# Window attention and softplus FFN: where the first block keeps its scores, and which engine forms the weights' lower parts

## The chip, the cores and the metric

The kernel runs on one core of one Trainium2 chip. The metric is device microseconds of one execution. Three runs of the kernel before gave a median of 1030.87 us (1030.74 to 1031.98).

## What is computed

Two stages follow each other. The first is attention over a window of 64 positions, for 8 batches, 8 heads, 576 positions and a head dimension of 64. The second is a feed-forward net (FFN) over the 4608 tokens, with 512 features and 2048 hidden units.

```python
scores = q @ k.transpose / sqrt(64)
scores = where((0 <= row - col) & (row - col < 64), scores, -1e9)
attn = softmax(scores)
x = (attn @ v) as [4608, 512]
h = x @ w_in
g = maximum(h, 0.0) + log1p(exp(-abs(h)))
out = (g @ w_out) as float32
```

The weights come as 64-bit floats, in 64-bit words.

## The kernel before, in words

**Blocks and pairs.** The 4608 tokens are worked on in 12 blocks of 384. In each block the attention is done for 4 head pairs (two heads of 64 make 128 features). The function `attention(g, hp)` is a generator: each `yield` ends a stage, and a list of events says at which point of the program the next stage is emitted. For the first two blocks (`by_pe`, L187) a stage list is: load q and k (L204, L206); load v (L226, L229); three score tiles, each a matmul (L254) and two masked copies with a row minimum on VectorE (L265); then, in one stage, the minimum over the two window ends (L271), six exponentials on ScalarE (L275), the sums' reciprocals (L280, L281), the scaling (L283), six transposes on TensorE (L290) and two copies out of PSUM (L291); then the product with v (L347), whose result is split into an upper part by ScalarE (L352) and a lower part by VectorE (L353). These two parts are `x`, what the FFN multiplies.

**Buffers of the first blocks.** The scores of a pair lie in the tile `st`, of which there are two (L246), so the third pair of a block can write its scores only when the first pair's transposes have read theirs. The k tiles (`kbd_s`), the v tiles (`v_ts`) and the two q tiles are also two each, taken in turn by `hp % 2`.

**Weights.** The 16 weight blocks (f = 0 to 15) are turned from 64-bit floats into a 32-bit value and then into an upper part `hi` and a lower part `lo` by `load_w(f)`: one DMA into `raws` (L166), ScalarE's |high word| scaled (L170), three bit operations on VectorE (L171, L172, L173), then for each of the two matrices ScalarE's rounded copy `hi` (L176) and GpSimd's difference `lo = w - hi` (L177). Blocks 0 to 11 take both matrices in one tile of 1024 elements per partition; blocks 12 to 15 take them one at a time, in tiles of 512. The tiles `raws` and `ws` of blocks 0 to 7 take turns in four pairs of spare buffers, `spare0` and `spare1`, `spare4` and `spare5`, `spare2` and `spare3`, `spare6` and `spare7`; blocks 8 to 11 use two of the pairs. Later the same spare buffers hold the finished parts of blocks 8 to 15.

**FFN.** A step (g, f) is `ffn_up` (12 matmuls L401, ScalarE L405 to L407, VectorE L409, L411, L412) and `ffn_down` (9 matmuls L422). The order of the passes is block 0 with f = 0 to 7, block 1 with all f, block 0 with f = 8 to 15, then blocks 2 to 11 with all f. After the first pass block 0's sum is put away in DRAM (`part`) through the tiles that also bring the last weight blocks in.

**Order of the work.** Each event has a number, and the events are emitted in the order of these numbers: the step n stands at 2n + 0.5 and 2n + 5.5, `load_w(f)` at `CONVERT[f]`, and a pair's stages at `BASE[g] + PACE[g] * hp` plus the offsets of `STG0` (blocks 0 and 1) or `STG` (the others). Up to event 100 the order on each engine's queue is not that of emission: a planner plays the program through with its own costs and takes, on each engine and on SP's DMA queue, the earliest emitted instruction that is ready in its simulated time. From event 100 on TensorE's order is that of emission. Whatever the plan, each queue then runs in its order on the chip.

```python
CONVERT = (-104, -98, -93, -88, -6, -3, 0, 3, 6, 8, 11, 13, 16, 18, 21, 24)
BASE = (-100, -10, 24)
PACE = (5, 4, 7)
STG0 = (-4.5, 0.5, 1, 2, 3, 4, 7, 8)
...
            if f == loaded:
...
    events.sort(key=lambda e: e[0])
```

**Start.** GpSimd zeroes parts of the k and v tiles (L115 to L118, L123: ten memsets), then builds the masks and the identity matrix (L127 to L146).

Of the kernel before, what the change touches and what calls it, by code (L numbers as in the profile page):

```python
# [8 lines left out]
F32 = mybir.dt.float32  # L9
# [4 lines left out]
ALU = mybir.AluOpType  # L14

P = 128
TB = 384
NJ = TB // P
WIN = 64
BIG = 1.0e9  # L20
CH = 64
# [1 line left out]

SPLIT = 8
DOWN = 5.5
CONVERT = (-104, -98, -93, -88, -6, -3, 0, 3, 6, 8, 11, 13, 16, 18, 21, 24)
BASE = (-100, -10, 24)
PACE = (5, 4, 7)
STG0 = (-4.5, 0.5, 1, 2, 3, 4, 7, 8)
# [10 lines left out]
def window_attention_softplus_ffn(  # L40
# [24 lines left out]
    nc = tc.nc  # L65
# [13 lines left out]
    att = ctx.enter_context(tc.tile_pool(name="att", bufs=1))  # L79
# [12 lines left out]
    NE = NF // 2  # L92
    w_first = [[cpool.tile([P, NE, DM], F32R, name=f"w{m}{i}") for i in range(2)] for m in range(2)]
    w_last = {}

    def spare(k, shape, dtype, name):
        return late.tile(shape, dtype, name=name, tag=f"spare{k}")

    def weight(m, i, f):

        if f < NE:
            return w_first[m][i][:, f, :]
        k = (f - NE) // 4
        if (m, i, k) not in w_last:
            w_last[m, i, k] = spare(4 * k + 2 * m + i, [P, 4, DM], F32R, f"w{m}{i}{k}")
        return w_last[m, i, k][:, f % 4, :]


    W = CH + P
# [2 lines left out]

    kbd_s = [att.tile([P, 2, CH + TB], F32, name="kbd", tag=f"k{i}") for i in range(2)]
    for t in kbd_s:
        nc.gpsimd.memset(t[D:P, 0, :], 0.0)  # L115
        nc.gpsimd.memset(t[0:D, 1, :], 0.0)
        nc.gpsimd.memset(t[0:D, 0, 0:CH], 0.0)
        nc.gpsimd.memset(t[D:P, 1, 0:CH], 0.0)  # L118

    v13 = cpool.tile([P, NCH, 2, 2, D], BF16, name="v13")  # L120
    v_ts = [att.tile([P, 2, NJ, P], F32, name="v_t", tag=n) for n in ("nat", "tr")]
    for t in v_ts:
        nc.gpsimd.memset(t[0:CH, 0, 0, :], 0.0)  # L123

# [23 lines left out]
    def load_w(f):  # L150


        if f < NE + 4:
            k = (0, 4, 2, 6)[f % 4] if f < NE else (4, 6)[f % 2]
            parts = [(spare(k, [P, 2, DM], w_words.dtype, "raws"), spare(k + 1, [P, 2, DM], F32, "ws"), 0, 2)]
        else:
            parts = [
                (
                    ff.tile([P, 1, DM], w_words.dtype, name="raw"),
                    att.tile([P, 1, DM], F32, name="wh", tag=("v_in", "v12")[m]),  # L160
                    m, m + 1,
                )
                for m in range(2)
            ]
        for raw, w, m0, m1 in parts:
            nc.sync.dma_start(raw, w_words[f][:, m0:m1, :])  # L166
            words = raw.bitcast(U32).rearrange("p m (n two) -> p two m n", two=2)
            low, high = words[:, 0, :, :], words[:, 1, :, :]
            wb = w.bitcast(U32)
            nc.scalar.activation(w, high.bitcast(F32), AF.Abs, scale=REBIAS)  # L170
            nc.vector.tensor_scalar(wb, wb, 3, None, ALU.logical_shift_left)  # L171
            nc.vector.scalar_tensor_tensor(wb, high, 0x80000000, wb, ALU.bitwise_and, ALU.bitwise_or)  # L172
            nc.vector.scalar_tensor_tensor(wb, low, 29, wb, ALU.logical_shift_right, ALU.bitwise_or)  # L173
            for m in range(m0, m1):
                hi, lo = [weight(m, i, f) for i in range(2)]
                nc.scalar.copy(hi, w[:, m - m0, :])  # L176
                nc.gpsimd.tensor_tensor(lo, w[:, m - m0, :], hi.bitcast(F32), ALU.subtract)  # L177


    xs = {}  # L180
# [2 lines left out]
    def attention(g, hp):  # L183
# [59 lines left out]
            nc.vector.tensor_tensor(k_lo, k_in, k_hi.bitcast(F32), ALU.subtract)  # L243
        yield

        st = att.tile([P, 2, NJ, W], F32, name="st", bufs=2)  # L246
        mn = att.tile([P, 2, NJ], F32, name="mn", bufs=2)
        sm = att.tile([P, 2 * NJ], F32, name="sm", bufs=2)
        for j in range(NJ):
# [12 lines left out]
            t = ORDER[g] * NJ + j  # L262
            m = mask_c if (t * P) % S == 0 else mask_b if (t * P) % S + P > S else mask
# [191 lines left out]
    for g in range(NB):  # L455
        for hp in range(NP):
            if g < 3:
                base = BASE[g] + PACE[g] * hp
            else:
                base = 2 * NF * (g - 1) + SHP * hp + SH  # L460
            stages = attention(g, hp)
            for at in STG if g >= 2 else STG0:
                events.append((base + at, lambda stages=stages: next(stages, None)))
    loaded = 0
    for n, (g, f, first, last) in enumerate(steps):
        if f == loaded:
            events.append((CONVERT[f], lambda f=f: load_w(f)))
            loaded += 1
        events.append((2 * n + 0.5, lambda g=g, f=f: ffn_up(g, f)))
        events.append((2 * n + DOWN, lambda step=steps[n]: ffn_down(*step)))  # L470
# [52 lines left out]
```

## Time and profile before

| | |
|---|---|
| median of 3 runs | 1030.87 us |
| the profiled execution, its own time | 1030.02 us |
| its span in the profile | 1028.2 us |
| TensorE (PE) busy | 974.8 us, 95% of the span |
| VectorE (DVE) busy | 802.6 us, 78% |
| ScalarE (ACT) busy | 742.0 us, 72% |
| GpSimd (POOL) busy | 61.8 us, 6% |
| granted TensorE clock, mean over the span | 0.976 of full |

The profile is of one execution. A row of a group view names the line, the engine, the operation and the tiles, then the busy time, the mean duration, and the idle time just ahead on that engine with what ended it. A row of a timeline gives start and duration, both in us. A row of windows gives, for one stretch of time, the busy time of each engine with its number of instructions, then the granted TensorE clock as a share of full speed and the DMA's share and rate.

### The profile page before, as it was taken

How to read it: one execution, taken by the hardware profiler on the slowest of the kernel's cores; microseconds unless marked ns; L12 is line 12 of the kernel's file. 1: busy time of each engine (PE TensorE's matmuls, PEld its weight loads, DVE VectorE, ACT ScalarE, POOL GpSimd, SP SyncE). 2: the span in 40 equal slices, each digit the busy share in tenths (PEclk: the TensorE clock that was granted, in tenths of full speed). 3: DMA queues.
4: the chain of work that ended last, by engine and by line, in shares of the span. 5: the costliest groups of instructions: out<-in, count | busy, mean ns of one | idle time of the engine just before them, and what ended most of it. 6: DMA issues, size and time to landing. Idle time of an engine off the chain costs nothing.

```text
span 1028.2 us, 16614 instructions
## 1 busy us (share of the span) xinstructions
PE 974.8 (95%) x5888; PEld 859.1 (84%) x5888; DVE 802.6 (78%) x1775; ACT 742.0 (72%) x1705; POOL 61.8 (6%) x56
## 2 busy tenths in 40 slices
PE   4559889999999999999999999999999999999998
PEld 2337778988888998998899899899989899889997
DVE  6998587797987888878878878878878887874332
ACT  5467477787877788778778778778878877865443
POOL 5365020000000000000000000000000000000000
PEclk8679989999999999999999999999999999999999
DMA  8662253375554456444444534534634635521000
GB/s 295 229 219 71 88 149 83 83 186 123 126 121 114 113 114 130 117 113 116 131 103 117 140 91 118 151 83 113 164 83 113 161 86 104 141 49 32 31 1 31
DMA packets 203155, 119.05 MB, mean 116 GB/s; under 512 B 130880, under 2 KB 195136, under 8 KB 201536
## 3 DMA queue, kind: packets, MB, share of 16 engines
q1 hardware_dynamic: 203072, 118.00, 45.4%
q8 instruction: 46, 0.75, 0.3%
q14 instruction: 37, 0.30, 0.1%
HBM read 76.28 MB, written 10.22 MB: 84 GB/s over the span
## 4 chain that ended last, share of the span: by engine, by line
PE 85%; DVE 9%; DMA 2%; ACT 1%; issue 1%; SPq 1%; DVEq 0%; ACTq 0%
PE ps_o L422 37%; PE ps_h L401 37%; PE ps_a L376 5%; PE ps_a L258 5%; DVE ws L172 2%; DVE ws L173 1%; DVE st L265 1%; DVE st L283 1%; DMA raws<-in_w_words_dram 1%; DVE ws L171 1%; DVE st L271 0%; DMA tr<-nat 0%; ACT st L275 0%; PE ps_a L254 0%; DVE sm L280 0%
## 5 line engine op out<-in xcount | busy, mean ns | idle before, releaser
L401 PE MATMUL ps_h<-x,w 128*128 128x384 f32 x2304 | 445.3, 340 | 7.6 <-ACT x L352 3.9
L422 PE MATMUL ps_o<-w,g 128*128 128x512 f32 x1728 | 435.5, 395 | 0.0
L401 PEld LDWEIGHTS ps_h<-x,w 128*128 128x128 f32 x2304 | 402.6, 189 | 22.5 <-ACT x L352 5.2
L422 PEld LDWEIGHTS ps_o<-w,g 128*128 128x128 f32 x1728 | 318.0, 188 | 57.7 <-ACT g L411 0.3
L405 ACT ACTIVATE u<-ps_h 128x384 f32<-128x384 f32 x192 | 93.9, 490 | 121.8 <-PE ps_h L401 118.8
L409 DVE SCALAR_TENSOR_TENSOR u<-ps_h,u 128x384 f32<-128x384 f32 x192 | 106.4, 554 | 70.5 <-ACT u L407 69.2
L275 ACT ACTIVATE st<-st,mn 128x128 f32<-128x128 f32 x288 | 111.9, 390 | 19.3 <-DVE st L271 19.3
L412 DVE TENSOR_TENSOR g<-u,g 128x384 fp32r<-128x384 f32 x192 | 106.6, 555 | 10.5 <-ACT g L411 8.6
L265 DVE CUSTOM_DVE_ANT_0 st<-ps_a,mask 128x192 f32<-128x192 f32 x216 | 69.4, 351 | 57.9 <-PE ps_a L258 45.4
L407 ACT ACTIVATE u<-u 128x384 f32<-128x384 f32 x192 | 100.3, 523 | 4.2
L406 ACT ACTIVATE u<-u 128x384 f32<-128x384 f32 x192 | 100.7, 526 | 3.2
L258 PE MATMUL ps_a<-k,q_hl 128*128 128x192 f32 x480 | 76.5, 283 | 0.0
L376 PEld LDWEIGHTS <-v 128*128 128x128 bf16 x1088 | 56.1, 98 | 22.9 <-issue 21.8
L376 PE MATMUL ps_a<-tr,v 128*128 128x128 bf16 (+1 forms) x1088 | 72.0, 213 | 0.2
L258 PEld LDWEIGHTS ps_a<-k,q_hl 128*128 128x128 f32 x480 | 66.6, 192 | 4.1 <-issue 0.5
L411 ACT CAST g<-u 128x384 fp32r<-128x384 f32 x112 | 57.0, 509 | 14.2 <-DVE u L409 13.5
L306 ACT CAST nat<-st 128x768 bf16<-128x768 f32 x40 | 33.2, 831 | 40.0 <-DVE st L304 40.0
L275 ACT ACTIVATION_READ_ACCUMULATOR st<-st,mn 128x1 f32 x288 | 53.9, 187 | 0.0
L381 ACT COPY xf<-ps_a 64x384 f32<-64x384 f32 x80 | 38.1, 477 | 20.3 <-PE ps_a L376 19.2
L283 DVE TENSOR_TENSOR st<-st,sm 128x768 f32<-128x768 f32 x48 | 47.6, 991 | 1.5
L382 DVE TENSOR_TENSOR xf<-ps_a,xf 64x384 f32<-64x384 f32 x80 | 43.9, 548 | 5.2 <-ACT xf L381 4.0
L325 DVE TENSOR_TENSOR v_in<-v_in,v 128x896 f32<-128x896 f32 x40 | 43.5, 1086 | 4.7 <-ACT v L324 4.7
(80 smaller groups left out, 868.0 us busy)
## 6 DMA issues: line engine op xcount, KB each, us to landing
k_in<-in_kT_dram SPq DMA_DIRECT2D x80, 224.0 KB, 3.9
v_in<-in_v_dram SPq DMA_DIRECT2D x80, 224.0 KB, 3.6
q_in<-in_qT_dram SPq DMA_DIRECT2D x84, 192.0 KB, 4.1
raws<-in_w_words_dram SPq DMA_DIRECT2D x12, 1024.0 KB, 6.0
out_dram<-raw SPq DMA_DIRECT2D x12, 512.0 KB, 2.8
raw<-in_w_words_dram SPq DMA_DIRECT2D x8, 512.0 KB, 4.3
out_dram<-raw SPq DMA_DIRECT2D x12, 256.0 KB, 2.6
v_t<-in_v_dram SPq DMA_DIRECT2D x16, 96.0 KB, 3.8
```

What stands on the lines that cost most here:

```text
L258: mm(spv[:, hh, :], q_hl[:, hh, js], part[:, hh, kc], start=(hh == 0 and i == 0), stop=(hh == 1 and i == 1), skip_group_check=True,)
L265: nc.vector.tensor_tensor_reduce(st[:, hh, j, :], spv[:, hh, :], m, QSCALE, 3.0e38, ALU.add, ALU.min, mn[:, hh, j : j + 1])
L275: nc.scalar.activation(sv[:, i, 0:P], sv[:, i, 0:P], AF.Exp, bias=mn[:, hh, j : j + 1], scale=-1.0, accum_out=sm[:, i : i + 1])
L283: nc.vector.tensor_tensor(pn, pn, sm.unsqueeze(2).to_broadcast([P, 2 * NJ, P]), ALU.mult)
L376: mm(av[:, osl], (v13 if s else v12)[:, c, hh, :, :], src, start=(i == 0), stop=(i == len(passes) - 1), skip_group_check=True,)
L401: mm(hv, weight(0, a, f)[:, c * P : (c + 1) * P], x[b][c], start=(i_mm == 0), stop=(i_mm == 3 * NC - 1))
L405: nc.scalar.activation(u, hv, AF.Abs)
L406: nc.scalar.activation(u, u, AF.Exp, scale=-1.0)
L407: nc.scalar.activation(u, u, AF.Ln, bias=1.0)
L409: nc.vector.scalar_tensor_tensor(gf, hv, 0.0, u, ALU.max, ALU.add)
L412: nc.vector.tensor_tensor(gt[1], gf, gt[0].bitcast(F32), ALU.subtract)
L422: mm(ops[g][j], gt[a][:, js], weight(1, b, f), start=(first and i == 0), stop=(last and i == 2),)
```

## The change

Four things are done.

- In block 0 each head pair gets a score tile of its own. The tiles are the spare buffers 0, 4, 2 and 6, the ones into which the raw words of weight blocks 0 to 3 are then loaded.
- So `load_w(0)` to `load_w(3)` are emitted later, each just behind the stage that reads the last scores of the pair whose buffer it takes (pair 0's at -96, the load at -95.5, and so on).
- The lower parts of all 16 weight blocks are formed by VectorE instead of GpSimd: 32 subtractions of 128x512.
- The ten memsets of the k and v tiles are issued on VectorE instead of GpSimd.

```diff
-CONVERT = (-104, -98, -93, -88, -6, -3, 0, 3, 6, 8, 11, 13, 16, 18, 21, 24)
+CONVERT = (-95.5, -90.5, -85.5, -80.5, -6, -3, 0, 3, 6, 8, 11, 13, 16, 18, 21, 24)
...
+    FIRST = (0, 4, 2, 6)
+
...
     for t in kbd_s:
-        nc.gpsimd.memset(t[D:P, 0, :], 0.0)
-        nc.gpsimd.memset(t[0:D, 1, :], 0.0)
-        nc.gpsimd.memset(t[0:D, 0, 0:CH], 0.0)
-        nc.gpsimd.memset(t[D:P, 1, 0:CH], 0.0)
+        nc.vector.memset(t[D:P, 0, :], 0.0)
+        nc.vector.memset(t[0:D, 1, :], 0.0)
+        nc.vector.memset(t[0:D, 0, 0:CH], 0.0)
+        nc.vector.memset(t[D:P, 1, 0:CH], 0.0)
...
     for t in v_ts:
-        nc.gpsimd.memset(t[0:CH, 0, 0, :], 0.0)
+        nc.vector.memset(t[0:CH, 0, 0, :], 0.0)
...
-            k = (0, 4, 2, 6)[f % 4] if f < NE else (4, 6)[f % 2]
+            k = FIRST[f % 4] if f < NE else (4, 6)[f % 2]
...
-                nc.gpsimd.tensor_tensor(lo, w[:, m - m0, :], hi.bitcast(F32), ALU.subtract)
+                nc.vector.tensor_tensor(lo, w[:, m - m0, :], hi.bitcast(F32), ALU.subtract)
...
-        st = att.tile([P, 2, NJ, W], F32, name="st", bufs=2)
+        if g == 0:
+
+            st = spare(FIRST[hp], [P, 2, NJ, W], F32, "st0")
+        else:
+            st = att.tile([P, 2, NJ, W], F32, name="st", bufs=2)
```

## Rows read from the trace of the kernel before

**Rows 1.** Windows over the whole span: busy time of each engine, clock, DMA.
```profile
0.00:97.00 97.00, 56.01 (x276) 38.15 (x277) 83.87 (x156) 55.60 (x140) 51.77 (x50) 0.79 0.65 213
97.00:135.00 38.00, 32.38 (x201) 26.86 (x199) 22.76 (x60) 19.50 (x55) 3.16 (x2) 0.95 0.30 94
135.00:200.00 65.00, 62.88 (x346) 55.92 (x347) 50.65 (x115) 50.73 (x116) 6.84 (x4) 0.97 0.43 104
...
200.00:1028.00 828.00, 823.52 (x5072) 738.21 (x5069) 645.31 (x1448) 616.13 (x1396) 0.00 (x0) 1.00 0.45 106
```

**Rows 2.** The chain that ended last, cut to 0 to 130 us, by line.
```profile
by line: DVE ws L172 14.7%; DVE ws L173 11.8%; PE ps_o L422 8.0%; PE ps_h L401 6.7%; DVE st L265 6.5%; issue 6.1%; DVE st L283 5.5%; DMA raws<-in_w_words_dram 5.2%; DVE ws L171 4.4%; PE ps_a L254 3.1%; DVE sm L280 3.1%; DMA part<-raw 2.8%; 
```

**Rows 3.** Timeline: the ends of the two blocks' attention, and the third pair's scores.
```profile
25.74 1.65 PE L254 MATMUL ps_a<-kbd,k_in 128*128 128x384 f32 x2
...
69.56 0.54 DVE L353 TENSOR_TENSOR x<-ps_o,x 128x384 fp32r<-128x384 f32 x1
...
134.46 0.45 ACT L352 CAST x<-ps_a 128x384 fp32r<-128x384 f32 x1
```

**Rows 4.** Timeline of TensorE: the first pair's scores, transposes and product with v.
```profile
4.50 4.18 PE L254 MATMUL ps_a<-kbd,k_in 128*128 128x384 f32 x6 [4.50 <-DMA kbd<-in_kT_dram]
...
22.83 1.51 PE L290 MATMUL ps_a<-ident,st 128*128 128x128 f32 x6 [7.85 <-ACT w L176]
24.27 1.54 PE L347 MATMUL ps_a<-pt,v_t 128*64 128x64 f32 x12
```

**Rows 5.** VectorE's groups by shape, 0 to 100 us.
```profile
L172 DVE SCALAR_TENSOR_TENSOR ws<-raws,ws 128x1024 uint32<-128x1024 uint32 x12 | 20.0, 1666 | 0.0
L173 DVE SCALAR_TENSOR_TENSOR ws<-raws,ws 128x1024 uint32<-128x1024 uint32 x12 | 16.1, 1338 | 0.0
L171 DVE TENSOR_SCALAR ws<-ws 128x1024 uint32<-128x1024 uint32 x12 | 11.9, 995 | 1.6 <-ACT ws L170 1.6
L283 DVE TENSOR_TENSOR st<-st,sm 128x768 f32<-128x768 f32 x6 | 7.3, 1221 | 0.1
...
L280 DVE TENSOR_SCALAR sm<-sm 128x6 f32<-128x6 f32 x6 | 4.2, 708 | 2.0 <-ACT st L275 2.0
```

**Rows 6.** Timeline of VectorE: single instructions, all but the last with GpSimd idle.
```profile
10.37 0.69 DVE L171 TENSOR_SCALAR ws<-ws 128x1024 uint32<-128x1024 uint32 x1 [1.61 <-ACT ws L170]
...
11.53 1.22 DVE L172 SCALAR_TENSOR_TENSOR ws<-raws,ws 128x1024 uint32<-128x1024 uint32 x1
...
17.18 0.17 DVE L280 TENSOR_SCALAR sm<-sm 128x6 f32<-128x6 f32 x1
...
25.52 0.94 DVE L283 TENSOR_TENSOR st<-st,sm 128x768 f32<-128x768 f32 x1
...
48.77 0.68 DVE L173 SCALAR_TENSOR_TENSOR wh<-raw,wh 128x512 uint32<-128x512 uint32 x1
...
71.11 2.28 DVE L172 SCALAR_TENSOR_TENSOR ws<-raws,ws 128x1024 uint32<-128x1024 uint32 x1
```

**Rows 7.** GpSimd: the window of its subtractions alone (L177), and two single rows.
```profile
0.00:100.00 100.00, 45.27 (x26) 0.80 0.63 207
...
69.49 2.82 POOL L177 TENSOR_TENSOR w<-ws,w 128x512 fp32r<-128x512 f32 x2 [2.49 <-ACT w L176]
93.63 1.29 POOL L177 TENSOR_TENSOR w<-wh,w 128x512 fp32r<-128x512 f32 x1
```

**Rows 8.** Timeline: the last memsets of the tiles on GpSimd, and VectorE's first instruction.
```profile
3.24 0.34 POOL L123 MEMSET v_t<- 64x128 f32 x2
...
7.56 0.36 DVE L265 CUSTOM_DVE_ANT_0 st<-ps_a,mask 128x192 f32<-128x192 f32 x1 [7.56 <-POOL mask_b L145]
```

**Rows 9.** SP's queue: one stretch in which it waits with two weight loads.
```profile
20.79 8.79 SPq L166 DMA_DIRECT2D raws<-in_w_words_dram  x2
```

**Rows 10.** From VectorE's last bit operation to GpSimd's subtraction, and the page's exponentials.
```profile
73.43 1.22 DVE L173 SCALAR_TENSOR_TENSOR ws<-raws,ws 128x1024 uint32<-128x1024 uint32 x1
...
75.38 2.94 POOL L177 TENSOR_TENSOR w<-ws,w 128x512 fp32r<-128x512 f32 x2 [3.07 <-ACT w L176]
...
L275 ACT ACTIVATE st<-st,mn 128x128 f32<-128x128 f32 x288 | 111.9, 390 | 19.3 <-DVE st L271 19.3
```

## The prediction

> **What bounds the kernel now.** I read the windows first. From 200 us on TensorE is busy 823.5 of 828 us at full clock, so nothing the change touches there can matter: all of it works in the first 200 us. There TensorE is busy 56.0 of 97, 32.4 of 38 and 62.9 of 65 us, part of it at a clock of 0.79 [rows 1]. The reader is to see that in the first stretch VectorE carries 83.9 of 97 us and TensorE waits. The chain says the same: up to 130 us its largest shares are VectorE's three bit operations on the weights (L172, L173, L171: 30.9% together) and the masks and scaling of the scores [rows 2].
>
> The order is the second thing to see. Block 0's x is complete only at 69.56 + 0.54 = 70.1 us, block 1's at 134.46 + 0.45 = 134.9 (its last lower part a little later) [rows 3]. Block 0's third pair scores at 25.74 us, right behind pair 0's transposes and product with v (22.83 to 25.8) [rows 3, 4], as two score tiles demand. VectorE fills that time with weights: by 100 us it has done 12 blocks' bit operations and GpSimd 26 subtractions, that is blocks 0 to 12, while the first pass needs 0 to 7 [rows 5, 7].
>
> **The subtractions.** Nothing in the trace shows this subtraction on VectorE. The nearest row is a 128x512 operation with two SBUF inputs of 32 bits: 0.68 us [rows 6]; below lies 0.17, the fixed price of a tiny operation, above 0.94, a subtraction-like operation of 768 elements [rows 6]. I take 0.68, the same shape and number of inputs. By 100 us that is 26 x 0.68 = 17.7 us, by 135 us 28 of them, 19.0 us. (The bounds make 28 cost 5 to 26 us.)
>
> What it frees: beside GpSimd's subtractions VectorE's own instructions are longer. L172 takes 1.22 us with GpSimd idle, and 2.28 at 71.11, while GpSimd's pair of subtractions runs from 69.49 to 72.31 [rows 6, 7]. The excess of the group means over such single rows is 12 x (1.666 - 1.22) = 5.4 for L172, 12 x (1.338 - 1.22) = 1.4 for L173, 12 x (0.995 - 0.69) = 3.7 for L171, 6 x (1.221 - 0.94) = 1.7 for L283, 6 x (0.708 - 0.17) = 3.2 for L280 [rows 5, 6]: 15.4 us, and groups not shown can only add. So the trade is nearly even on VectorE, 3.6 us dearer by 135 us.
>
> The Trainium skill, page SBUF — State Buffer, section Who interferes with whom, says that VectorE and GpSimd share a pair of ports as an exclusive lock, and that the one that comes second blocks for the whole instruction. By that rule I estimate a gain of up to 26 x 1.29 = 33.5 us of VectorE time instead of 15.4, which would make the sum some 18 us better; the trace agrees on single instructions, which lose 1.06 us, and not on the sum.
>
> GpSimd loses too: its subtractions take 45.27 / 26 = 1.74 us each, against 1.29 for one late in the stretch [rows 7]. The waiting is split between the two, and I keep the measured 15.4.
>
> **The memsets.** Ten memsets leave GpSimd, where the last two end at 3.58 us; VectorE waits for GpSimd's masks until 7.56 [rows 8]. VectorE has nothing else to do then, so they cost nothing there as long as that cover lasts (if it is gone, at most the 3.58 us within which all ten ran on GpSimd). GpSimd's masks come earlier by up to as much; TensorE's first score tile is there from about 4.50 + 4.18 / 6 = 5.2 us [rows 4], so VectorE may start at 5.2 instead of 7.56: 2.4 us gained, bounds 0 and 2.4.
>
> **The score tiles and the later weight loads.** With four tiles the third and fourth pair no longer wait for the transposes of the first two. What they wait for next is TensorE: a pair takes 4.18 + 1.51 + 1.54 = 7.2 us in the early rows [rows 4], so four pairs take 29, and x of block 0 can't be complete before about 4.5 + 29 + 1 = 34 us. With a couple of weight blocks on VectorE in between (1.22 + 1.22 + 0.69 + 2 x 0.68 = 4.5 us each) I expect 40 to 45, against 70. The raw words of blocks 0 to 3 load only after the transposes of their pair, so conversion starts near 17 us instead of 9: harmless while VectorE has attention to do, and I put 4 us of new idle time on it. The loads stand in SP's queue, where v and k loads can be stuck behind them, as happened for 8.79 us before [rows 9]; this wait is now for transposes rather than for conversions, and I cost it at nothing beyond those 4 us.
>
> An earlier x does not by itself shorten the front, since VectorE must do its work first. So the sum runs over VectorE, to the state "block 1's x complete and the first pass done", 135 us now. Busy time up to there 83.87 + 22.76 = 106.6 [rows 1]; minus 15.4, plus 19.0: 110.2. Idle time up to there is 13.1 + 15.2 = 28.4. The 15.2 fall after 97 us, when TensorE runs the whole first pass as one lump and VectorE has nothing pressing; with x of block 0 some 28 us earlier the first pass spreads out beside the conversion, and I take 3 of them as left. The 13.1 become 13.1 - 2.4 + 4, and I add 3 for subtractions that wait for ScalarE's `hi` (below). That is 20.7 of idle time and a state at 130.9: 4 us gained.
>
> The rest comes from order. Weight blocks 8 to 13 were done before this state and are not needed for it; they crowded in because attention was blocked. Six blocks are 27 us of VectorE. I take half as postponed, 13.5 us, and they have a place: from 135 to 200 us VectorE is idle 14.3 of 65 us [rows 1]. The state then lies at 117.4, 17.6 us earlier, and from there on TensorE is the bound as now. The profiled execution took 1030.02 us, 0.85 below the median of the runs shown; 1030.0 - 17.6 = 1012.4, or 1013 against the median. With none postponed it is 1027, with all of them 1000.
>
> **The rivals.**
> - *More than that.* All six blocks are postponed and the conversion of later ones fits under the second pass: 31 us, 1000 (988 to 1003 with the clock's share, which stands at 0.79 in the first 97 us [rows 1]). Against it: 27 us don't fit in the 14.3 of idle time. Or half are postponed, as forecast, and each of GpSimd's subtractions had held VectorE up for its whole 1.29 us [rows 7]: 26 x 1.29 - 15.4 = 18.1 us more, 1013 - 18 = 995. For this speaks L172's 2.28, against it that the group means show an excess of 15.4 only. Chance 0.13 together, little of it the second. By the rule of the Trainium skill's page SBUF — State Buffer cited above it would be the second.
> - *It evens out.* The scores come early but the planner still lets the weights crowd in, or weight loads in SP's queue hold up the loads of pairs 2 and 3. VectorE is then only 3.6 us dearer and starts 2.4 earlier: 1026 to 1035, about 1031. For it: 8.79 us of such a stretch in the trace [rows 9]; against it: pair 2's matmuls waited with TensorE idle 7.85 us just ahead of the transposes [rows 4]. Chance 0.17.
> - *VectorE waits for ScalarE, slower.* GpSimd waited for `hi` at no cost; VectorE, with everything queued behind, does not. L173 ends at 74.65 and the subtraction could start at 75.38, 0.73 us later, with ScalarE free [rows 10]. Where `hi` stands behind a pair's six exponentials it is 6 x 0.39 = 2.3 us more [rows 10]. Over 14 blocks the mechanism decides from 17.6 / 14 = 1.3 us a block; at 2 us a block it costs 28 against 17.6, 1041, at 3 us 1055. Behind the waiting subtraction stand masks and scaling of the next pairs, for which TensorE waits. Against it: the planner knows this dependency and places other work between. Chance 0.18.
>
> **How the numbers follow.** The forecast has 0.52, with a range of its own from 1003 to 1026. About 0.2%, 2 us, is what a measurement of this kernel can tell from no change. Faster is the forecast, the larger gain and a part of the even case: 0.52 + 0.13 + 0.05 = 0.70. Same is 0.07 of the even case. Slower is 0.05 of it and the 0.18: 0.23. For 8 in 10 the range takes in the forecast, the better end to 998 (0.04), the even case, and the slower one up to 1036, a wait of about 1.6 us a block (0.07).
>
> **What would show it.** Right: no L177 on GpSimd; L172 close to 1.22 us in the mean and L280 near 0.17; 32 subtractions of about 0.68 us on VectorE; block 0's third pair scoring before pair 0's transposes, x of block 0 complete before 45 us; block 1's x near 117; blocks 8 to 13 partly converted after that. Wrong: x of block 1 still near 135, with VectorE as busy; VectorE idle ahead of the subtractions, ended by ScalarE's L176, beyond some 18 us in all; or ScalarE long idle ahead of L170 for raw words that come late.

## The result, and the profile after

The changed kernel takes 1034.1 us (median of 20 runs, 1028.98 to 1039.08), the kernel before 1031.26 (20 runs, 1029.9 to 1032.73): a ratio of 1.0027, 95% interval 1.0014 to 1.0039. It is slower by about 3 us where 1013 was forecast. Lines from `def spare` on stand 2 further down in the new file, those from `st` on 6.

The engines' busy time on the page of the changed kernel (1035.78 us, span 1034.0):

```profile
PE 982.4 (95%) x5888; PEld 867.2 (84%) x5888; DVE 802.4 (78%) x1817; ACT 741.9 (72%) x1705; POOL 3.9 (0%) x14
```

GpSimd's work is gone but for 3.9 us (61.8 before). TensorE runs the same 5888 matmuls but is busy 7.6 us longer, so it idles 51.6 us of its span against 53.4 before. What was lost is not idle time but clock (0.970 of full in the mean of the span, 0.976 before). The windows (columns as in [rows 1]) show where:

```profile
0.00:97.00 97.00, 70.94 (x354) 51.74 (x355) 81.14 (x199) 57.39 (x146) 3.94 (x14) 0.82 0.65 213
97.00:135.00 38.00, 24.01 (x127) 19.60 (x126) 29.01 (x59) 19.90 (x51) 0.00 (x0) 0.76 0.41 116
135.00:200.00 65.00, 59.83 (x319) 52.95 (x318) 44.71 (x105) 46.84 (x111) 0.00 (x0) 0.96 0.38 94
```

Up to 97 us TensorE does 354 matmuls instead of 276: the early score tiles work. From 97 to 135 it does 127 instead of 201, at a granted clock of 0.76 instead of 0.95. So by 135 us the two kernels stand even, with 481 matmuls and 477 before; it is from 135 to 200 us that the changed kernel falls behind, with 319 matmuls instead of 346. VectorE is busy 81.14 + 29.01 = 110.15 us by 135 us; the forecast's sum, before anything is postponed, said 110.2. The two blocks' last parts of x, on VectorE's timeline:

```profile
55.20 0.55 DVE L359 TENSOR_TENSOR x<-ps_o,x 128x384 fp32r<-128x384 f32 x1
...
133.40 0.56 DVE L359 TENSOR_TENSOR x<-ps_a,x 128x384 fp32r<-128x384 f32 x1 [0.69 <-ACT x L358]
```

Block 0's x is complete 14 us earlier than before (55.8 against 70.1), block 1's only 1.5 us (134.0 against 135.5). VectorE's groups, 0 to 135 us, answer to [rows 5]:

```profile
L179 DVE TENSOR_TENSOR w<-ws,w 128x512 fp32r<-128x512 f32 x24 | 15.6, 681 | 0.7 <-ACT w L178 0.7
L175 DVE SCALAR_TENSOR_TENSOR ws<-raws,ws 128x1024 uint32<-128x1024 uint32 x12 | 14.6, 1216 | 0.0
L174 DVE SCALAR_TENSOR_TENSOR ws<-raws,ws 128x1024 uint32<-128x1024 uint32 x12 | 14.5, 1215 | 0.0
L173 DVE TENSOR_SCALAR ws<-ws 128x1024 uint32<-128x1024 uint32 x12 | 8.2, 687 | 4.1 <-ACT ws L172 4.0
...
L173 DVE TENSOR_SCALAR wh<-wh 128x512 uint32<-128x512 uint32 x6 | 2.5, 424 | 4.7 <-ACT wh L172 4.7
L286 DVE TENSOR_SCALAR sm<-sm 128x6 f32<-128x6 f32 x8 | 1.3, 163 | 5.3 <-ACT st L281 5.3
```

The prices are the forecast ones: the subtraction 0.68 us, the bit operations 1.22 and 0.69, the tiny L286 0.16. The subtractions (L179) wait 0.7 us for ScalarE in all, so the slower rival's mechanism did not occur. Much of the idle time, 8.7 us, stands ahead of L173 instead, where VectorE waits for ScalarE's first step on the weights. ScalarE's waits up to 135 us (total, times, longest) say for what:

```profile
ACT ws L172 <- DMA raws<-in_w_words_dram: 10.6, 6, 4.6
...
ACT wh L172 <- DMA raw<-in_w_words_dram: 7.3, 4, 4.4
```

That is 17.9 us for raw words not yet there; before it was 8.5 + 3.2 = 11.7. What stands behind such a wait in ScalarE's queue waits too. Two places on ScalarE's timeline, at the third pair of block 0 and the fourth of block 1:

```profile
41.95 1.12 ACT L172 ACTIVATE ws<-raws 128x1024 f32<-128x1024 f32 x1 [4.62 <-DMA raws<-in_w_words_dram]
42.97 0.47 ACT L297 COPY pt<-ps_a 128x384 f32<-128x384 f32 x1
...
129.31 0.66 ACT L172 ACTIVATE wh<-raw 128x512 f32<-128x512 f32 x1 [4.44 <-DMA raw<-in_w_words_dram]
129.88 0.46 ACT L297 COPY pt<-ps_a 128x384 f32<-128x384 f32 x1
```

And TensorE's timeline at the same two places, the transposes (L296) and the product with v (L353) that needs their copy:

```profile
37.67 1.49 PE L296 MATMUL ps_a<-ident,st 128*128 128x128 f32 x6
...
43.49 1.54 PE L353 MATMUL ps_a<-pt,v_t 128*64 128x64 f32 x12 [3.06 <-ACT pt L297]
...
125.06 1.51 PE L296 MATMUL ps_a<-ident,st 128*128 128x128 f32 x6 [6.22 <-DVE st L289]
130.39 2.46 PE L353 MATMUL ps_a<-pt,v_t 128*64 128x64 f32 x24 [3.82 <-ACT pt L297]
```

The copy of the transposed scores could have run at about 39 and 126.5 us, where the transposes end. It stood behind a weight block that was still loading, and TensorE idled 3.06 and 3.82 us for it. The Trainium skill, page Perfetto Trace Analysis, section Tensor Engine Instruction (MATMUL, LD_WEIGHTS), says that ScalarE and VectorE execute strictly first in, first out; these rows agree.

### The profile page after: what moved, and what is told of

Same layout as the page of the kernel before. It is cut to its first block, busy times and chain, and to the rows that moved or that the text cites. A ratio compares the mean times of both kernels' runs of the same rounds, so it can differ in the third digit from the quotient of the medians.

```text
span 1034.0 us, 16622 instructions
## 1 busy us (share of the span) xinstructions
PE 982.4 (95%) x5888; PEld 867.2 (84%) x5888; DVE 802.4 (78%) x1817; ACT 741.9 (72%) x1705; POOL 3.9 (0%) x14
## 4 chain that ended last, share of the span: by engine, by line
PE 88%; DMA 4%; DVE 4%; ACT 2%; issue 1%; SPq 0%; ACTq 0%; DVEq 0%
PE ps_h L407 37%; PE ps_o L428 37%; PE ps_a L382 5%; PE ps_a L264 5%; DMA raws<-in_w_words_dram 1%; PE ps_a L260 1%; PE ps_a L353 1%; ACT st L281 1%; DVE ws L175 1%; DMA tr<-nat 1%; DMA part<-raw 0%; DVE w L179 0%; DVE st L271 0%; DMA v_in<-in_v_dram 0%; DVE ws L174 0%
## 5 line engine op out<-in xcount | busy, mean ns | idle before, releaser
L407 PE MATMUL ps_h<-x,w 128*128 128x384 f32 x2304 | 450.5, 343 | 21.5 <-DVE u L415 7.3
L407 PEld LDWEIGHTS ps_h<-x,w 128*128 128x128 f32 x2304 | 407.5, 191 | 37.5 <-ACT w L178 12.3
L281 ACT ACTIVATE st<-st,mn 128x128 f32<-128x128 f32 x288 | 111.9, 390 | 16.3 <-DVE st L277 16.3
L271 DVE CUSTOM_DVE_ANT_0 st<-ps_a,mask 128x192 f32<-128x192 f32 x216 | 69.7, 351 | 51.9 <-PE ps_a L264 50.7
```

Of the source, the lines that this page charges most:

```text
L271: nc.vector.tensor_tensor_reduce(st[:, hh, j, :], spv[:, hh, :], m, QSCALE, 3.0e38, ALU.add, ALU.min, mn[:, hh, j : j + 1])
L281: nc.scalar.activation(sv[:, i, 0:P], sv[:, i, 0:P], AF.Exp, bias=mn[:, hh, j : j + 1], scale=-1.0, accum_out=sm[:, i : i + 1])
L407: mm(hv, weight(0, a, f)[:, c * P : (c + 1) * P], x[b][c], start=(i_mm == 0), stop=(i_mm == 3 * NC - 1))
```

## The experiments

All ratios are to the kernel before, on the same chip in the same batch; a bracket is its 95% interval. 18 kernels ran, and none leaves work out.

**Parts of the change alone.** Two kernels start from the one before: one gets the score tiles and the later loads, the other only the subtractions.

```diff
-                nc.gpsimd.tensor_tensor(lo, w[:, m - m0, :], hi.bitcast(F32), ALU.subtract)
+                nc.vector.tensor_tensor(lo, w[:, m - m0, :], hi.bitcast(F32), ALU.subtract)
```

Two start from the changed one: the scores lie in the other spare of each pair, or the raw words are loaded through GpSimd's queue.

```diff
-            st = spare(FIRST[hp], [P, 2, NJ, W], F32, "st0")
+            st = spare(FIRST[hp] + 1, [P, 2, NJ, W], F32, "st0")
...
-            nc.sync.dma_start(raw, w_words[f][:, m0:m1, :])
+            nc.gpsimd.dma_start(raw, w_words[f][:, m0:m1, :])
```

> The score tiles and the later loads of weight blocks 0 to 3 alone; subtractions and memsets stay on GpSimd. Theory L (the raw words of blocks 0 to 3 now come late, and ScalarE's conversion of them stands in its queue ahead of the attention's copies): ScalarE still waits 8 us or more for raw words ahead of its first conversions between 20 and 60 us, block 0's x is complete near 55 us, and the time is 1031 to 1037, no better than the whole change. Rival S (the subtractions on VectorE are what eats the gain): 1022 to 1028, since VectorE then has 19 us less to do.

> The subtractions on VectorE alone, everything else as before. Theory L: no late words, so the exchange of 19.0 us of subtractions for some 15 us of contention is all there is: 1028 to 1034. Rival S: the subtractions cost on the path to block 1's x: 1035 or more.

> The whole change, but the scores of block 0 lie in the spare buffers of the converted words (1, 5, 3, 7) instead of those of the raw words (0, 4, 2, 6), so the raw words of blocks 0 to 3 can be loaded before the scores are read. Theory L: ScalarE's waits for raw words in the first 60 us fall from about 10 us to under 4, block 0's x is complete before 48 us instead of 55.8, and the time falls to 1022 to 1029. Rival Q (what delays the attention is SP's queue, where its loads stand behind weight loads that wait for a buffer): the waits of SP for conversions stay as long, x of block 1 stays near 133, the time stays within 1031 to 1036.

> The whole change, but the raw words of all weights are loaded through GpSimd's queue, so no load of the attention stands behind a weight load. Rival Q: v, q and k loads of block 1 issue as soon as their own buffers are free, block 1's x is complete by 120 us instead of 133, and the time falls to 1018 to 1027. Theory L alone: the raw words of blocks 0 to 3 come as late as before, block 0's x stays near 55 us and the time within 1030 to 1036.

Measured: score tiles 1026.11 us, 0.9956 [0.9942, 0.9971]; subtractions 1022.86, 0.9924 [0.9909, 0.9939]; scores in the other spare 1030.5, 1.0004 [0.9991, 1.0018]; GpSimd's queue 1041.32, 1.0108 [1.0093, 1.0124]. Each half helps alone, by the ratios 4.5 and 7.8 us, and together with the memsets they cost 3. Taking the waiting loads out of SP's queue does not mend it: through GpSimd's the kernel is slower still. Only the score tiles fall into a range that was named, and the reason given for that range, that the subtractions eat the gain, does not fit the second kernel, where they gain; the other three lie outside both of their ranges. The planner also gave each of these kernels an order of its own, so they do not yet separate the parts.

**Memsets, and weights that come later.** Each half alone got the ten memsets on VectorE too. And weights were postponed in the changed kernel: by their event numbers, or the last two blocks by an order on ScalarE alone.

```diff
-CONVERT = (-95.5, -90.5, -85.5, -80.5, -6, -3, 0, 3, 6, 8, 11, 13, 16, 18, 21, 24)
+CONVERT = (-95.5, -90.5, -85.5, -80.5, -6, -3, 0, 3, 18, 20, 22, 24, 26, 28, 30, 32)
```

```diff
-            nc.scalar.activation(w, high.bitcast(F32), AF.Abs, scale=REBIAS)
+            first = nc.scalar.activation(w, high.bitcast(F32), AF.Abs, scale=REBIAS)
+            if f >= NF - 2:
+                tc.add_manual_dep(
+                    first.ins, x_last[0].ins.name,
...
```

> Score tiles, later loads and memsets as changed, the subtractions on GpSimd: the change without its subtractions. If the memsets do nothing, as theory W and rival V both say, it is within 3 us of the 1026.1 of the score tiles alone. If the memsets are what hurts beside the score tiles (they start VectorE earlier and so give another plan), it is 1030 or more.

> Subtractions and memsets on VectorE, the scores and the loads as before. If the memsets do nothing: within 3 us of the 1022.9 of the subtractions alone. If they hurt: 1027 or more.

> The whole change, with weight blocks 8 to 15 emitted behind all of block 1's attention (at 18, 20, 22, 24, 26, 28, 30 and 32 instead of 6, 8, 11, 13, 16, 18, 21 and 24). Theory V (these blocks crowd in on VectorE ahead of block 1's attention): by block 1's x VectorE has formed at most 20 lower parts instead of 29, x is complete by 122, and the time falls to 1018 to 1027. Theory W: they are taken early anyway, because their words are there and the attention waits for ScalarE and its loads; 26 or more lower parts are formed by then and the time stays within 1030 to 1037.

> The whole change, with one constraint on the order of ScalarE's queue: the conversions of weight blocks 14 and 15 come behind the cast of block 1's last x. Theory W (in the changed kernel ScalarE stands still for words of block 14, which wait for the first pass's sum to be put away, with block 1's last copies queued behind): the 3.8 us hole of TensorE ahead of the last pair's product with v goes, block 1's x is complete by 130.5 instead of 134.0, and the time falls by 3 to 7 us, to 1027 to 1031. Rival V (VectorE's sum of work sets that state, whatever ScalarE does): x of block 1 stays past 132 and the time within 1032 to 1036.

Measured: score tiles with memsets 1038.77, 1.0081 [1.0058, 1.0104]; subtractions with memsets 1035.81, 1.0049 [1.0031, 1.0066]; late blocks 1018.19, 0.9882 [0.9866, 0.9898]; last two behind 1025.29, 0.9946 [0.9927, 0.9965]. The late blocks seemed to settle it: weights that crowd in. Yet only the time met that theory: 26 lower parts are formed by block 1's x (121.3 us), where it asked for at most 20. And ten memsets of together 2.5 us, which VectorE runs while it has nothing else to do, cost 12.7 and 13 us, and no row of the trace holds such a price. What the memsets also change is the planner's order, on every queue.

**The order held fast.** In the next kernel each queue's order is written out, so that nothing differs from the subtractions-alone kernel but the engine of the ten memsets. `PINNED` lists each engine's instructions as the planner had ordered them there.

```diff
+    by_name = {i.name: i for i in tc.nc.cur_bb.bb.instructions}
+    for steps_of in PINNED.values():
...
+            if behind is not None:
+                tc.add_manual_dep(
+                    ins, behind.name,
+                    mybir.DependencyInfo(mybir.DependencyClass.NoSync, mybir.DependencyReason.DATA), reason="order",
+                )
+            behind = ins
```

Beside it ran the changed kernel with `nc.gpsimd.memset` as before, the same with the late `CONVERT`, and the kernel before with late blocks 8 to 15.

> Subtractions on VectorE and the ten memsets on VectorE, as in p_lo_mem (1035.8), but every engine's queue and SP's stands in the order that the planner made for p_lo (1022.9, memsets on GpSimd); only the ten memsets change their engine. Theory M (the memsets cost nothing by themselves; moving them makes the planner choose another order, and that order costs the 13 us): 1021 to 1025, PE's gap of 19.7 us near 55 us gone. Rival E (the memsets on VectorE cost by what they do there): 1031 to 1037.

> The whole change, except that the ten memsets stay on GpSimd. Theory M1 (the memsets' move costs about 13 us whatever else is done, as it did in both pairs so far): 1019 to 1024, faster than before. Rival I (what the memsets' move costs belongs to the one plan it was made in; the whole change is slow because the weights crowd in ahead of block 1, and that stays): 1030 to 1036, block 1's x at 130 us or later.

> The whole change with weight blocks 8 to 15 emitted late (as in a_late, 1018.2), and the ten memsets left on GpSimd. If the memsets' price adds to every plan: 1004 to 1008. If the late emission already takes away what the other order cost: 1016 to 1020.

> The kernel before, with weight blocks 8 to 15 emitted late and nothing else. If the postponement alone is worth what it was worth on top of the change (1034 to 1018, 16 us): 1013 to 1018. If it needs the four score tiles or GpSimd's freed port, because before it the attention of block 0 is blocked and VectorE fills that time with weights at no cost: 1026 to 1032, block 0's x still near 70 us.

Measured: order held 1023.67, 0.9935 [0.9917, 0.9953]; without the memsets 1033.03, 1.0022 [1.001, 1.0033]; that with late blocks 1022.66, 0.9936 [0.9913, 0.9958]; before with late blocks 1033.34, 1.0024 [1.0014, 1.0034]. So the memsets by themselves cost nothing that these runs can tell: 1035.8 against 1023.7 is order alone. The gap that was to vanish shrank from 19.7 us to 14.3, so the time was right and that detail not. Leaving the memsets on GpSimd doesn't mend the changed kernel, which refutes the theory that their move costs 13 us everywhere: their price belongs to one plan. With late blocks the kernel without them is even the slower one (1022.66 against 1018.19), outside both of its ranges. And late blocks make the kernel before 2.5 us slower.

**Which theory, with the order held.** In one kernel the changed kernel keeps its own order on every queue, and only the conversions of blocks 14 and 15 move back. In two others only the subtractions move, in the order of the kernel before and in that of the score-tiles kernel. A last one shifts the late `CONVERT` by two events (16 to 30 instead of 18 to 32).

> The changed kernel with every engine's queue and SP's in the order that its own planner made (1034.1), except the instructions that convert weight blocks 14 and 15: these stand behind block 1's last upper part of x. TensorE's order is the same to the last matmul. Theory W (weights that crowd in ahead of block 1's x cost the gain): 1022 to 1029, block 1's x at 126 to 130. Rival P (the gain of a_order, 1025.3, came from the other order of the rest): 1032 to 1036, block 1's x still at 132 or later.

> The kernel before with every queue in its own order; only the 32 subtractions go from GpSimd to VectorE, placed by the planner between the fixed others. The forecast's term (nearly even on VectorE, 3.6 us dearer): 1030 to 1036. If the 15.4 us of freed port count for more than the subtractions, because they lie on the path and the subtractions do not: 1021 to 1027, as p_lo with its own order (1022.9).

> Score tiles, later loads and the subtractions on VectorE, memsets on GpSimd, every queue in the order made for p_scores (1026.1, subtractions on GpSimd); only the 32 subtractions are added on VectorE. a_nomem, with the same work in its own order, took 1033.0. If the 7 us between them are the other order: 1023 to 1029. If they are the subtractions on VectorE: 1031 to 1036.

> The changed kernel with blocks 8 to 15 emitted late, each two events earlier than in a_late (1018.2). Theory W: what counts is that they stand behind block 1's attention, so 1015 to 1023 again. Rival P (a_late met a lucky order): anywhere from 1022 to 1036.

Measured: blocks 14 and 15 back 1040.23, 1.0082 [1.0059, 1.0105]; subtractions in the order of before 1025.23, 0.9941 [0.9925, 0.9956]; score tiles and subtractions in the order of score tiles 1017.28, 0.9864 [0.9849, 0.9879]; shifted late blocks 1022.7, 0.9932 [0.991, 0.9955]. The first refutes my theory: block 1's x does come earlier, at 127.5 instead of 134.0 us, and TensorE's wait for the copy at the fourth pair is gone, yet the time is 6 us longer. The cost turns up behind it, where the postponed work meets the second pass:

```profile
135.00:200.00 65.00, 56.24 (x285) 49.81 (x285) 41.65 (x90) 41.14 (x99) 0.00 (x0) 0.87 0.34 79
```

TensorE is busy 56.24 of 65 us at a clock of 0.87 there, against 59.83 at 0.96 in the changed kernel. The third says it from the other side. Score tiles and subtractions together gain 1.36%, 14 us, in the order that was made for the score tiles; in the order that the planner makes for the two together (1033.03 above) they gain nothing. The shifted late blocks fit both of their ranges and decide nothing. Late blocks on top of the change do make it faster than the kernel before in all three kernels of this kind (1018.2, 1022.7, 1022.7), but each has an order of its own, and how much of that is the lateness was not separated.

**The whole change in another order.** The last two: every instruction of the changed kernel, memsets included, in the order of the score-tiles kernel, the 32 subtractions placed by the planner between the others; and the changed kernel with three orders on TensorE, so that the first pass's matmuls last longer beside block 1's attention.

```diff
+    UP, DN = {(0, 5): (1, 1)}, {(0, 3): (1, 1), (0, 6): (1, 2)}
...
+                if i_mm == 0:
+                    behind((g, f), UP, made)
...
+                if i == 0 and j == 0:
+                    behind((g, f), DN, made)
```

> All instructions of the changed kernel, the ten memsets on VectorE too, with every queue in the order made for p_scores; the 32 subtractions are placed by the planner between the fixed others. If the order alone costs the gain: 1015 to 1020, as a_nomem_pin (1017.3), block 1's x at 120 to 123. If the memsets add something in this order: 1025 or more.

> The changed kernel in its planner's hands, with three orders on TensorE alone: the first pass's sixth step multiplies up only behind the transposes of block 1's second pair, its fourth step multiplies down behind the same, its seventh step down behind those of the third pair. So 60 instead of 72 matmuls up stand ahead of the second pair's transposes (60 in the kernel before and in p_scores), and 60 instead of 69 down ahead of the third's. Theory C (the first pass spent early leaves TensorE without work beside block 1's last pairs): 1017 to 1027, PE's busy time from 97 to 135 us 27 or more instead of 24.0. Rival D (what is bad lies in VectorE's and SP's order): 1030 to 1038.

Measured: the whole change in the other order 1017.83 us, 0.9881 [0.9864, 0.9897]; the orders on TensorE 1038.19, 1.0079 [1.0064, 1.0094]. The first is the work of the changed kernel to the last instruction, on the same engines, 16.3 us faster (15 by the two ratios). It beats the kernel before by some 12 us, as do the late blocks (1018.19) and, by 14, the kernel without memsets in that order (1017.28); their intervals overlap. The engines' busy time on its page:

```profile
PE 972.5 (96%) x5888; PEld 861.4 (85%) x5888; DVE 801.0 (79%) x1817; ACT 740.4 (73%) x1705; POOL 4.0 (0%) x14
```

And its windows, which answer to [rows 1]:

```profile
0.00:97.00 97.00, 69.30 (x370) 52.09 (x371) 87.14 (x208) 61.38 (x160) 3.96 (x14) 0.86 0.68 222
97.00:135.00 38.00, 30.92 (x169) 26.19 (x168) 32.95 (x82) 26.08 (x67) 0.00 (x0) 0.87 0.44 132
135.00:200.00 65.00, 64.23 (x379) 57.54 (x378) 47.80 (x107) 50.31 (x115) 0.00 (x0) 1.00 0.41 89
```

Of the 18.8 us between the two profiled spans (1034.0 and 1015.2) 9.9 are TensorE's busy time, the same matmuls at a lower mean clock (0.970 against 0.980), and 8.9 its idle time. VectorE does 120.1 us of work by 135 us instead of 110.2. At the third pair of block 0 and the fourth of block 1 ScalarE's timeline now has the copy ahead of the weights:

```profile
36.97 0.48 ACT L297 COPY pt<-ps_a 128x384 f32<-128x384 f32 x1 [0.99 <-PE ps_a L296]
38.61 1.13 ACT L172 ACTIVATE ws<-raws 128x1024 f32<-128x1024 f32 x1 [1.16 <-DMA raws<-in_w_words_dram]
...
114.71 0.48 ACT L297 COPY pt<-ps_a 128x384 f32<-128x384 f32 x1 [2.39 <-PE ps_a L296]
117.69 0.48 ACT L358 CAST x<-ps_a 128x384 fp32r<-128x384 f32 x1 [2.50 <-PE ps_a L353]
...
118.80 0.68 ACT L172 ACTIVATE wh<-raw 128x512 f32<-128x512 f32 x1
```

ScalarE's waits for raw words fall from 17.9 us to 7.5, and TensorE's wait for the copy falls with them. The row of TensorE's waits up to 135 us, in the changed kernel:

```profile
PE ps_a L353 <- ACT pt L297: 7.4, 3, 3.8
```

And the same work in the other order:

```profile
PE ps_a L353 <- ACT pt L297: 0.5, 2, 0.3
```

The kernel with orders on TensorE misses: TensorE is busy 27.65 us from 97 to 135 us, as that theory asked, and the time grows. TensorE's early use of the first pass is not the fault, or not alone.

## Why the prediction was wrong

**Subtractions, right in the price, too dear in the sum.** With the order of before held, VectorE has the same instructions ahead of block 1's x, and 28 subtractions more. Its work up to there, in the kernel before and with only the subtractions moved (columns as in [rows 1]):

```profile
0.00:135.50 135.50, 88.89 (x476) 65.47 (x476) 107.13 (x216) 75.60 (x194) 54.93 (x52) 0.83 0.55 179
...
0.00:131.50 131.50, 87.97 (x476) 65.72 (x476) 105.09 (x244) 75.81 (x195) 6.48 (x24) 0.84 0.55 184
```

The 28 subtractions are 18.39 us of the 105.09, so 20.4 us came free, and the trade is 2.0 us cheaper (forecast 15.4 free, 3.6 dearer). The forecast had left out L271, whose mean falls from 763 to 554 ns: 1.7 us. Block 1's x comes 4.0 us earlier, the other half of that by less idle time, and the kernel is 6.1 us faster. One wait that goes is that of ScalarE's first step on a block for GpSimd, which still read the buffer. In the kernel before, up to 135 us:

```profile
ACT ws L170 <- POOL w L177: 5.6, 2, 3.8
```

But ScalarE's waits for raw words grow meanwhile from 11.7 to 15.4 us, so this wait alone does not explain the gain; what else goes into the 6.1 us is not shown. By the Trainium skill's rule (SBUF — State Buffer, section Who interferes with whom) up to 33.5 us would have come free; 20.4 did, so the measurement decides for the smaller figure, though that the loss ends with GpSimd's work, L174 at 1.215 us in the mean instead of 1.666, agrees with it. That the changed kernel's 110.15 us meet the forecast's 110.2 is luck: more came free than forecast, and the memsets' 2.5 us, which the forecast put at nothing, stand against it.

**Memsets, right as a price.** With the order held they add 0.8 and 0.5 us by the medians, 1.1 and 1.8 by the ratios, inside the intervals. VectorE's first scores come at 6.42 us instead of 7.56; 5.2 was forecast.

**Block 0's x at 40 to 45.** It came at 55.8, and at 49.5 in the better order. "A couple of weight blocks in between" were four whole ones and two halves, and VectorE stood idle 3.71 us there for the load that ends at 41.95.

**The step that failed** is the one on order. The forecast wrote "I take half as postponed, 13.5 us", for weight blocks 8 to 13, and nothing was postponed: 29 lower parts are formed when block 1's x is complete, 28 in the kernel before. Nothing in the change moves these blocks (`CONVERT` is as before from block 4 on); the term rested on what the planner would do, and the planner took as many weights ahead of x as before. VectorE up to that point, in the changed kernel and in the better order:

```profile
0.00:134.00 134.00, 93.96 (x476) 70.34 (x476) 109.28 (x256) 76.29 (x196) 3.94 (x14) 0.81 0.58 185
...
0.00:118.80 118.80, 86.31 (x476) 65.24 (x476) 104.74 (x249) 73.64 (x193) 3.96 (x14) 0.87 0.62 203
```

The state was forecast at 117.4 us and came at 134.0. Of these 16.6 us, 12.6 are VectorE's work (109.3 us instead of 110.2 - 13.5 = 96.7): the postponement that did not come. The other 4.0 are idle time, 24.7 us instead of 20.7, with the waits for raw words in it that were costed "at nothing beyond those 4 us". In the better order nothing is postponed either (28 lower parts by 118.8 us), but VectorE idles only 14.0 us, and block 1's x is complete at 118.8. That this lies so near the forecast's 117.4 is luck: 8.1 us more work and 6.7 us less idle time than forecast.

**From the state to the time.** The clause "from there on TensorE is the bound as now" failed too. At that point all three kernels have done 476 matmuls and have 5412 left (the first pass is done by then in all three: the last copy of its sum ends on VectorE at 125.5 us before, at 120.0 in the changed kernel, at 112.5 in the better order). For the rest the kernel before takes 892.7 us, the changed kernel 900.0, the better order 896.4. So behind its state the changed kernel loses 7.3 us more, 2.5 of them longer busy time and 4.8 idle, while the second pass, block 1's, runs beside block 2's attention; the better order loses 3.7, which is why its x is 16.7 us earlier than before and its time only 13.0 (profiled executions, 1030.02 and 1017.03). The forecast for the profiled execution was 1012.4 and the measured time 1035.78: 12.6 + 4.0 + 7.3 make up the 23.4 us between them but for 0.5, by which the state before lies behind the 135 us that the forecast took.

**The rivals.** "It evens out" named 1031 at 0.17, and came nearest in time. Its reason, that "the planner still lets the weights crowd in", describes what happened, but the weights crowd in just as much in the better order, so it is not what cost the gain. For the other reason, loads of pairs 2 and 3 held up in SP's queue, TensorE's waits show no sign: behind the first 4.6 us it waits for no load of k or v. The 8.79 us of SP's queue [rows 9] and the sign to look for, ScalarE idle ahead of its step on the weights, stood in the text; neither had a price.

**What stays open.** That order alone costs the 16.3 us is shown. Two waits of ScalarE's queue, about 7 us of TensorE's waiting together, are seen in the one order and not in the other. The second was taken away with the order otherwise held, when blocks 14 and 15 moved back: x came 6.5 us earlier and the time grew by 6 us, so taking it away in that manner gained nothing. The first was not tried alone. Which other differences make up the rest, and why the planner prefers that order, is not settled; TensorE's order moved alone made it slower as well.

## What to carry to other kernels

Where a planner makes the order, a change is two changes: what its instructions cost, and a new order on every queue, which here was worth 12 to 16 us; measure a part once with the order held before you believe or discard it. A gain that counts on a planner to postpone work needs an edit that postpones it. In an in-order queue, price the first instruction that waits for a load by what stands behind it: a weight conversion put one place ahead of a copy kept TensorE waiting 3 to 4 us each time. Price also where the conversion goes instead: with two blocks moved behind block 1's x the wait went, and the time grew by 6 us. When an engine gives up slow work, count the buffers it releases sooner as well as the port it frees.

## What was not expected of the hardware

The same 5888 matmuls are 974.8, 982.4 or 972.5 us busy, by the order of the work around them. The granted clock of 0.76 that the changed kernel shows from 97 to 135 us is a mean of two levels. From 115 us on, in steps of 5:

```profile
115.00:120.00 5.00, 3.84 (x34) 2.54 (x32) 4.94 (x15) 1.20 (x3) 0.00 (x0) 1.00 0.45 152
120.00:125.00 5.00, 0.00 (x0) 0.00 (x0) 2.45 (x6) 3.08 (x13) 0.00 (x0) 0.83 0.95 276
125.00:130.00 5.00, 1.51 (x6) 1.14 (x6) 1.72 (x3) 0.69 (x2) 0.00 (x0) 0.50 0.52 164
```

TensorE has nothing to do from 120 to 125 us, the clock falls in that stretch, and the matmuls behind it run at 0.50, the lower level. The busy share of a stretch does not give its clock: from 97 to 135 us TensorE is busy 30.9 of 38 us at 0.87 in the better order, and 29.5 at 0.96 without the memsets in that order. About half of the difference between the two orders, 9.9 of 18.8 us, shows as longer busy time and not as idle time, and a comparison of idle time alone would have missed it.
